# Small work of the attention phase moved from VectorE to GpSimd, and TensorE's unread products taken out

## The chip, the cores and the metric

The kernel runs on one core of one Trainium2 chip. A core has five engines with a queue of instructions each: TensorE (PE, matrix products into PSUM banks), VectorE (DVE), ScalarE (ACT), GpSimd (POOL) and SyncE (SP), which here issues nearly all DMAs. The engines run beside each other and wait for one another through semaphores; each keeps its own order. The metric is the time of one launch on the device, in microseconds (us), as the median of several runs.

## The reference

The kernel computes an attention block with normalised queries and keys, then a feed-forward block with a squared relu, all in float32:

```python
# q, k, v: (8, 12, 448, 64); g_q, g_k: (64,); w_in: (768, 2048); w_out: (2048, 768)
def rmsnorm(x, g):
    return x / np.sqrt(np.mean(x * x, axis=-1, keepdims=True) + 1e-06) * g
scores = np.matmul(rmsnorm(q, g_q), rmsnorm(k, g_k).transpose(0, 1, 3, 2)) / np.sqrt(64)
attn = np.exp(scores - np.max(scores, axis=-1, keepdims=True))
attn = attn / (np.sum(attn, axis=-1, keepdims=True) + 1e-09)
x = np.matmul(attn, v).transpose(0, 2, 1, 3).reshape(3584, 768)
h = np.maximum(x @ w_in, 0.0)
out = h * h @ w_out
```

## The kernel before

The kernel takes two heads at a time (a "pair" `i`; 48 pairs, 6 for each batch). The first 12 pairs (two batches, `alone(i)`) go through attention before any feed-forward product can start; this is the first phase. Afterwards four feed-forward units, of two batches each, run with the attention of later pairs set in between their products. The feed-forward products use a form with 7 products in place of 8, so each weight tile and each x tile also needs sums and differences of its quarters ("quarter sums", "first differences"). The weights come in as words that ACT and DVE split and join (`convert`); the first four tiles of them (two of `w_in`, two of `w_out`) are made in the first phase, by `early`.

The start, before the branch on the size of the gains, and after it (cut):

```python
        gains = psum.tile([P, 1], F32, name="gains")
        nothing = psum.tile([P, P], F32, name="nothing")
        for _ in range(10):
            nc.tensor.matmul(nothing, lhsT=ident, rhs=ident, start=True, stop=True)
        ...
        idle(2)          # products of the identity into bank 5, read by nothing
        turn(0, 1)       # transposes of k, on TensorE
        idle(5)
        turn(0, 0)       # of q, after it has been scaled
        idle(5)
        for x in range(2):
            rows.normalize_first(1, x, new_acc()[:, 0 : 4 * P])
```

Normalising is a sum of squares (`square` on ACT or POOL, `add` on DVE), a power of -1/2 on POOL, and for q a scaling on POOL (line 221), which the next `turn` on TensorE waits for.

The denominators of a pair in the first phase: TensorE adds the weights with columns of ones, into two blocks of 32 rows for each head (line 488), so two partial sums have to be added over partitions:

```python
    def take_sums(i):
        inverse[i] = io.tile([P, S], F32, name="inverse", tag="squares", bufs=1)
        nc.vector.transpose(inverse[i], sums_bank(i))                              # 516

    def invert(i):
        columns = inverse[i].rearrange("p (t n) -> p t n", n=SIDE)
        few = columns[:, :, 0:1]
        if alone(i) or shift:
            other, both = new_few(), new_few()
            for n in range(P // SIDE):
                nc.vector.tensor_copy(out=other[ts(n, SIDE)], in_=few[ts(n ^ 1, SIDE)])   # 525
            nc.vector.tensor_tensor(out=both, in0=few, in1=other, op=ALU.add)             # 526
            few = both
        ...
        nc.vector.reciprocal(out=by, in_=few)                                      # 531
        nc.vector.transpose(columns, by.to_broadcast([P, S // SIDE, SIDE]))        # 532
    # finish(i): xT = values' bank * inverse, on DVE (544); then begin_forms(c) for the second batch
```

Two PSUM banks hold values and sums of the pairs by turns. The visit of a pair in the first phase has two halves, `n` = 0 and 1; `begin` makes two quarter sums and, when it is time, converts a piece of weights:

```python
    def make_sum():
        if sums_to_make:
            to, left, right, op = sums_to_make.popleft()
            next(sum_engines).tensor_tensor(out=to, in0=left, in1=right, op=op)    # 904, DVE and POOL by turns
        elif forms_to_store:
            nc.sync.dma_start(*forms_to_store.popleft())

    early = deque(2 + 2.4 * n for n in range(ahead + 1))     # ahead = 16

    def begin(step):
        for _ in range(2):
            make_sum()
        while early and early[0] <= step:
            early.popleft()
            convert()
            end_join()

    def visit_alone(i, n):
        step = i * 2 * VISITS + 2 * n                        # VISITS = 2
        if n == 0:
            load_v(i)
            weigh_slots(i, n)                                # scores, exponentials (401, 409)
            turn(i + 1, 0); turn(i + 1, 1)
            square(i + 2, 0, new_acc()); square(i + 2, 1, new_acc(), nc.gpsimd)
            begin(step)
            normalize(i + 2, 0)
            attend(i - 1, range(NJ))                         # weights times values (475)
        else:
            weigh_slots(i, n)
            normalize(i + 2, 1)
            begin(step)
            ...
            load_qk(i + 4)
            attend(i - 1, (NJ,))
            add_weights(i - 1, range(NJ + 1))                # 488
            take_sums(i - 1)
            invert(i - 1)
            finish(i - 1)
        begin(step + 1)
```

In the later phases POOL has added up the weights of a pair beforehand, and `denominators(i)` multiplies their sum by ones (505) and calls `take_sums`. It is called from the pair's visit, or, in the first feed-forward unit and for every other pair, half a visit ahead of it:

```python
                    if n and first and x > 1 and i % 2 == 0 and not shift:
                        denominators(i - 1)
                run(COST * x / unit)                         # feed-forward products up to here
                ...
                    visit_among(i, n)                        # denominators(i - 1) here, if not yet made
```

Of the kernel before, what the change touches and what calls it, by code (L numbers as in the profile page):

```python
# [13 lines left out]
F32 = mybir.dt.float32  # L14
# [3 lines left out]
ALU = mybir.AluOpType  # L18
# [3 lines left out]
P = 128  # L22
# [4 lines left out]
SIDE = 32  # L27
# [9 lines left out]
@with_exitstack  # L37
def kernel(
    ctx: ExitStack,
    tc: tile.TileContext,  # L40
    q: bass.AP,
    k: bass.AP,
    v: bass.AP,
    g_q: bass.AP,
    g_k: bass.AP,
    moe_w_in: bass.AP,
    moe_w_out: bass.AP,
    out: bass.AP,
):

    nc = tc.nc
    D = q.shape[3]
    const = ctx.enter_context(tc.tile_pool(name="const", bufs=1))
    wide = const.tile([P, P + D], F32, name="wide")
    ident = wide[:, 0:P]  # L60
    ones = const.tile([P, D], F32, name="ones")
    minus_half = const.tile([P, 1], F32, name="minus_half")
    g = const.tile([P, 1], F32, name="g")
    g_most = const.tile([1, 1], F32, name="g_most")
    bounded = const.tile([1, 1], I32, name="bounded")
    rows = Rows(nc, SimpleNamespace(io=const, small=const), q, k, minus_half)
    with (
        tc.tile_pool(name="early", bufs=1) as early,
        tc.tile_pool(name="gains", bufs=1, space=bass.MemoryType.PSUM) as psum,
        tc.manual_schedule(engines=ENGINES),  # L70
    ):
        g_rows = early.tile([1, 2, D], F32, name="g_rows")
        for n, row in enumerate((g_q, g_k)):
            nc.scalar.dma_start(g_rows[:, n], row.rearrange("(one d) -> one d", one=1))
        rows.load_full(0, 0, nc.sync)
        rows.load_rest(0, 0, nc.scalar)
        rows.load_full(0, 1, nc.sync)
        rows.load_rest(0, 1, nc.sync)
        for x in range(2):
            rows.load_full(1, x, nc.sync)  # L80
        nc.vector.memset(ones, 1.0)
        nc.vector.memset(minus_half, -0.5)
        nc.scalar.activation(early.tile([1, 1], F32, name="some"), ones[0:1, 0:1], AF.Exp)
        make_identity(nc, ident)
        nc.gpsimd.tensor_copy(out=wide[:, P : P + D], in_=ident[:, 0:D])
        nc.vector.tensor_tensor(out=g_rows[:, 0], in0=g_rows[:, 0], in1=g_rows[:, 1], op=ALU.mult)
        nc.vector.tensor_reduce(
            out=g_most, in_=g_rows[:, 0], axis=AX.X, op=ALU.max, apply_absolute_value=True
        )
        nc.vector.tensor_scalar(  # L90
            out=bounded, in0=g_most, scalar1=MOST_G, scalar2=None, op0=ALU.is_le
        )
        gains = psum.tile([P, 1], F32, name="gains")

        nothing = psum.tile([P, P], F32, name="nothing")
        for _ in range(10):
            nc.tensor.matmul(nothing, lhsT=ident, rhs=ident, start=True, stop=True)
        for e in range(2):
            nc.tensor.matmul(
                gains[ds(e * D, D), :], lhsT=g_rows[:, 0], rhs=ones[0:1, 0:1], start=True, stop=True  # L100
            )
        for x in range(2):
            rows.normalize_first(0, x, early.tile([P, 2 * P + 2 * P], F32, name=f"squares{x}"))
        nc.scalar.mul(g, gains, D**-0.5)
    flag = nc.values_load(bounded, min_val=0, max_val=1)
    with tc.If(flag > 0) as either:
        program(tc, rows, v, g, wide, ones, moe_w_in, moe_w_out, out, shift=False)
    with either.Else():
        program(tc, rows, v, g, wide, ones, moe_w_in, moe_w_out, out, shift=True)
# [118 lines left out]
def program(ctx, tc, rows, v, g, wide, ones, moe_w_in, moe_w_out, out, shift):  # L228

    nc = tc.nc  # L230
# [18 lines left out]
    psum = ctx.enter_context(tc.tile_pool(name="psum", bufs=1, space=bass.MemoryType.PSUM))  # L249
# [3 lines left out]
    ident = wide[:, 0:P]  # L253
# [260 lines left out]
    def take_sums(i):  # L514
        inverse[i] = io.tile([P, S], F32, name="inverse", tag="squares", bufs=1)
        nc.vector.transpose(inverse[i], sums_bank(i))  # L516
# [4 lines that stand above are left out]
        new_few = lambda: small.tile([P, S // SIDE, 1], F32, name="few", tag="few", bufs=3)  # L521
        if alone(i) or shift:
            other, both = new_few(), new_few()
            for n in range(P // SIDE):
                nc.vector.tensor_copy(out=other[ts(n, SIDE)], in_=few[ts(n ^ 1, SIDE)])
            nc.vector.tensor_tensor(out=both, in0=few, in1=other, op=ALU.add)
            few = both
        if shift:
            nc.vector.tensor_scalar(out=few, in0=few, scalar1=1e-9, scalar2=None, op0=ALU.add)
        by = new_few()  # L530
        nc.vector.reciprocal(out=by, in_=few)
        nc.vector.transpose(columns, by.to_broadcast([P, S // SIDE, SIDE]))
# [34 lines left out]
    def less(engine, dst, left, right):  # L567
        return lambda: engine.tensor_tensor(out=dst, in0=left, in1=right, op=ALU.subtract)
# [12 lines left out]
    def begin_forms(c):  # L581

        if c < NK:
            b11, b12, t1 = xts.pop((0, c)), xts.pop((1, c)), new_x()
            less(nc.vector, t1, b12, b11)()
            forms[0, c] = {"11": b11, "T1": t1, "T3": b12}
            return
        c -= NK
        b21, b22, t2, t4 = xts.pop((0, c + NK)), xts.pop((1, c + NK)), new_x(), new_x()
        some = forms[0, c]  # L590
        less(nc.vector, t2, b22, some["T1"])()
        less(nc.gpsimd, some["T3"], b22, some["T3"])()
        less(nc.gpsimd, t4, t2, b21)()
        some.update({"21": b21, "22": b22, "T2": t2, "T4": t4})
# [303 lines left out]
    sum_engines = cycle((nc.vector, nc.gpsimd))  # L898

    def make_sum():  # L900

        if sums_to_make:
            to, left, right, op = sums_to_make.popleft()
            next(sum_engines).tensor_tensor(out=to, in0=left, in1=right, op=op)
        elif forms_to_store:
            nc.sync.dma_start(*forms_to_store.popleft())

# [66 lines left out]
# [7 lines that stand above are left out]
# [35 lines left out]
    def visit_alone(i, n):  # L1016
        step = i * 2 * VISITS + 2 * n
        if n == 0:
            load_v(i)
            if i and shift:  # L1020
                attend_all(i - 1)
            weigh_slots(i, n)
            turn(i + 1, 0)
            turn(i + 1, 1)
            square(i + 2, 0, new_acc())
            square(i + 2, 1, new_acc(), nc.gpsimd)
            begin(step)
            normalize(i + 2, 0)
            if i and not shift:
                attend(i - 1, range(NJ))  # L1030
# [4 lines that stand above are left out]
            if in_blocks(i + 2):  # L1035
                store_q(i + 2)
                load_blocks(i + 2, 0)
                load_blocks(i + 2, 1)
            load_qk(i + 4)
            if i and not shift:  # L1040
                attend(i - 1, (NJ,))
                add_weights(i - 1, range(NJ + 1))
                forget(i - 1, range(NJ + 1))
                take_sums(i - 1)
                invert(i - 1)
                finish(i - 1)
            if not alone(i) and not shift:
                additions(i)
        begin(step + 1)

    def put_in_order(i):
        for x in range(2):
# [76 lines left out]
    with tc.manual_schedule(engines=ENGINES):  # L1129
        if shift:  # L1130
            rows.scale(0, 1, nc.gpsimd)
        def idle(number):
            for _ in range(number):
                nc.tensor.matmul(banks[5][:, 0:P], lhsT=ident, rhs=ident, start=True, stop=True)

        idle(2)
        turn(0, 1)
        idle(5)
        turn(0, 0)
        idle(5)  # L1140
        for x in range(2):
            rows.normalize_first(1, x, new_acc()[:, 0 : 4 * P])
        if shift:
# [1 line left out]
        for i in range(len(pairs) + 1):  # L1145
            for n in range(1 if whole(i) else VISITS):
# [8 lines left out]
                if i < last:  # L1155
                    for some in (1, 0) if whole(i) else (1 - n,):
                        turn_among(i + 1, some)
                    if n or whole(i):
                        tasks.append(lambda i=i: load_qk(i + 4))
                    if n and first and x > 1 and i % 2 == 0 and not shift:  # L1160
                        denominators(i - 1)
                run(COST * x / unit)
                if x == unit:
# [43 lines left out]
```

## Time and profile before

| What | Value |
|---|---|
| time, median of 3 runs | 1438.16 us (1435.96 to 1438.75) |
| span of the profiled execution | 1436.9 us |
| first phase: from the start to the first feed-forward product (L663) | 136.5 us |
| x W_in products (L663), busy | 514.6 us |
| products with W_out (L744, two groups of left operands) | 266.5 and 203.9 us |
| scores (L401) and values (L475), busy over the whole run | 162.5 and 102.0 us |
| POOL's power (L206), 96 times | 146.6 us |

A row of the profile's groups has line, engine, operation, output and inputs by the program's names, shape and type, count; then busy time and the mean length of one in ns; then the idle time of the engine just before it and what ended it. "L401" is line 401 of the kernel. PEld is the loading of weights into TensorE, beside its products. A product in float32 shows as two records. The chain of waits is followed back from the last instruction: at each step to what released it.

### The profile page before, as it was taken

How to read it: one execution, taken by the hardware profiler on the slowest of the kernel's cores; microseconds unless marked ns; L12 is line 12 of the kernel's file. 1: busy time of each engine (PE TensorE's matmuls, PEld its weight loads, DVE VectorE, ACT ScalarE, POOL GpSimd, SP SyncE). 2: the span in 40 equal slices, each digit the busy share in tenths (PEclk: the TensorE clock that was granted, in tenths of full speed). 3: DMA queues.
4: the chain of work that ended last, by engine and by line, in shares of the span. 5: the costliest groups of instructions: out<-in, count | busy, mean ns of one | idle time of the engine just before them, and what ended most of it. 6: DMA issues, size and time to landing. Idle time of an engine off the chain costs nothing.

```text
span 1436.9 us, 15452 instructions
## 1 busy us (share of the span) xinstructions
PE 1417.4 (99%) x4976; PEld 694.9 (48%) x4976; DVE 671.4 (47%) x1269; ACT 585.2 (41%) x1102; POOL 646.1 (45%) x568
## 2 busy tenths in 40 slices
PE   9999999999999999999999999999999999999997
PEld 5333444444444445445454544545454455555554
DVE  5997366877868523334242532334243341132313
ACT  6774566557554343432424334341432303212130
POOL 5667654746647654354535644453451502011110
PEclk9999999999999999999999999999999999999999
DMA  5765346666567654534425464344422232313122
GB/s 146 188 192 155 66 119 174 184 181 173 178 193 230 195 135 96 174 88 127 127 52 176 113 209 112 86 141 93 153 70 88 94 153 78 117 48 126 39 88 80
DMA packets 309280, 188.12 MB, mean 131 GB/s; under 512 B 265796, under 2 KB 293316, under 8 KB 300996
## 3 DMA queue, kind: packets, MB, share of 16 engines
q1 hardware_dynamic: 308896, 186.97, 44.5%
q8 instruction: 41, 0.67, 0.2%
q14 instruction: 51, 0.42, 0.1%
q10 hardware_dynamic: 292, 0.07, 0.0%
HBM read 144.57 MB, written 42.40 MB: 130 GB/s over the span
## 4 chain that ended last, share of the span: by engine, by line
PE 93%; DVE 2%; SPq 1%; DMA 1%; ACT 1%; issue 1%; POOL 1%; DVEq 0%; POOLq 0%
PE bank L663 36%; PE bank L744 29%; PE bank L475 10%; PE bank L401 9%; PE bank L715 5%; PE bank L505 2%; PE bank L488 1%; SPq L161 1%; PE bank L366 1%; DVE acc L785 0%; DMA words<-in_moe_w_out_dram 0%; DVE in_sb L882 0%; DVE in_sb L858 0%; DMA qk<-in_k_dram 0%; DVE in_sb L878 0%
## 5 line engine op out<-in xcount | busy, mean ns | idle before, releaser
L663 PE MATMUL bank<-xT,in_sb 128*128 128x448 f32 x1344 | 514.6, 542 | 0.0
L663 PEld LDWEIGHTS bank<-xT,in_sb 128*128 128x128 f32 x1344 | 253.2, 190 | 258.8 <-issue 248.3
L785 DVE TENSOR_TENSOR acc<-acc,bank 128x384 f32<-128x384 f32 x324 | 174.1, 550 | 216.7 <-PE bank L744 173.7
L744 PE MATMUL bank<-out_sb,hid 128*128 128x384 f32 x768 | 266.5, 487 | 0.0
L683 DVE TENSOR_TENSOR hid<-bank,part 128x448 f32<-128x448 f32 x128 | 76.9, 622 | 313.0 <-PE bank L663 310.2
L409 ACT ACTIVATE wT<-bank,rr 128x448 f32<-128x448 f32 x288 | 160.8, 631 | 127.2 <-PE bank L401 80.9
L744 PE MATMUL bank<-out_sb,sums 128*128 128x384 f32 x576 | 203.9, 490 | 3.0 <-DVE acc L785 2.9
L206 POOL TENSOR_TENSOR rr<-ms,minus_half 128x8 f32<-128x8 f32 (+1 forms) x96 | 146.6, 1527 | 112.5 <-DVE ms L199 105.4
L744 PEld LDWEIGHTS bank<-out_sb,hid 128*128 128x128 f32 x768 | 145.7, 190 | 103.3 <-issue 1.4
L428 POOL TENSOR_TENSOR sum<-wT 128x448 f32<-128x448 f32 x72 | 83.8, 1183 | 213.3 <-PE bank L505 213.3
L699 POOL TENSOR_TENSOR sums<-hid 128x384 f32<-128x384 f32 x32 | 32.1, 1002 | 310.4 <-ACT hid L685 310.4
L428 POOL TENSOR_TENSOR sum<-sum,wT 128x448 f32<-128x448 f32 (+1 forms) x144 | 163.7, 1161 | 10.8 <-ACT wT L409 8.1
L401 PE MATMUL bank<-qT,kT 64*128 64x448 f32 (+1 forms) x768 | 162.5, 569 | 0.6 <-ACT wT L409 0.3
L684 ACT ACTIVATE hid<-hid 128x448 f32<-128x448 f32 x128 | 73.3, 573 | 189.7 <-DVE hid L683 189.7
L744 PEld LDWEIGHTS bank<-out_sb,sums 128*128 128x128 f32 x576 | 108.0, 190 | 86.7 <-DVE acc L785 7.5
L670 ACT COPY part<-bank 128x448 f32<-128x448 f32 x128 | 67.6, 528 | 177.4 <-PE bank L663 177.4
L401 PEld LDWEIGHTS bank<-qT,kT 64*128 64x128 f32 (+1 forms) x768 | 54.4, 172 | 102.2 <-issue 66.4
L475 PE MATMUL bank<-wT,vt 128*64 128x448 f32 x480 | 102.0, 546 | 0.0
L516 DVE STREAM_TRANSPOSE inverse<-bank 128x448 f32<-128x448 f32 x48 | 30.9, 643 | 119.4 <-PE bank L505 111.8
L715 PE MATMUL bank<-out_sb,hid 128*128 128x384 f32 x256 | 85.6, 488 | 0.0
L339 ACT ACTIVATE qT<-qT,g 128x448 f32<-128x448 f32 x34 | 22.6, 665 | 143.0 <-DVE qT L337 143.0
L685 ACT ACTIVATE hid<-hid 128x448 f32<-128x448 f32 x128 | 73.8, 577 | 4.1
(87 smaller groups left out, 1189.5 us busy)
## 6 DMA issues: line engine op xcount, KB each, us to landing
out_sb<-out_forms SPq DMA_DIRECT2D x24, 1536.0 KB, 9.5
in_sb<-in_forms SPq DMA_DIRECT2D x24, 1344.0 KB, 6.1
words<-in_moe_w_in_dram SPq DMA_DIRECT2D x32, 384.0 KB, 3.8
words<-in_moe_w_out_dram SPq DMA_DIRECT2D x32, 384.0 KB, 3.8
out_forms<-out_sb SPq DMA_DIRECT2D x8, 1536.0 KB, 6.8
in_forms<-in_sb SPq DMA_DIRECT2D x8, 1344.0 KB, 6.0
qk<-in_q_dram SPq DMA_DIRECT2D x96, 96.0 KB, 3.0
qk<-in_k_dram SPq DMA_DIRECT2D x96, 96.0 KB, 2.7
```

The lines of the kernel that those rows point to most:

```text
L206: self.nc.gpsimd.tensor_tensor(out=self.rr[i][:, x, 0 : self.count(i)], in0=ms, in1=self.minus_half.to_broadcast(list(ms.shape)), op=ALU.pow,)
L401: nc.tensor.matmul(sc[some], lhsT=turned[p, 1][r, keys], rhs=turned[p, 0][r, :], start=True, stop=True,)
L409: nc.scalar.activation(new_weights((i, m), e), sc, AF.Exp, scale=rows.rr[i][:, 1, 2 * m + e : 2 * m + e + 1],)
L428: nc.gpsimd.tensor_tensor(out=sums[i, e][some], in0=left[some], in1=weights[key_of(i, m), e][some], op=ALU.add)
L475: nc.tensor.matmul(values_bank(i)[ds(e * D, D), :], lhsT=lasts[i % 2][mine, e, :] if m == NJ else values[i][:, m, e, :], rhs=weights[key_o ...
L663: nc.tensor.matmul(ps, lhsT=w_sb[:, IN.index(left), c, :], rhs=forms[u, c][right], start=first and c == 0, stop=c == NK - 1, skip_group_ch ...
L683: nc.vector.tensor_tensor(out=dst, in0=left, in1=right, op=op)
L684: nc.scalar.activation(dst, dst, AF.Relu)
L685: nc.scalar.activation(dst, dst, AF.Square)
L715: nc.tensor.matmul(ps, lhsT=flat[a][:, t, ds(NT * P, P)], rhs=w_sb[t][:, 2 * a + half, :], start=(a, t) == parts[0], stop=(a, t) == parts[-1],
L744: nc.tensor.matmul(ps, lhsT=lefts[left][:, t, ts(tt, P)], rhs=w_sb[t][:, OUT.index(right), :], start=first and t == 0, stop=t == 1, skip_g ...
L785: nc.vector.tensor_tensor(out=acc, in0=acc, in1=ps, op=ALU.add)
```

## The change

It takes out the products of the identity that nothing reads, at the start. In the first phase, it gives POOL the exchange of the partial sums over partitions and their addition (in `invert`), the quarter sums of the weights while `early` still has entries, and the first differences of the x tiles of the first two batches (`begin_forms`, three times); all of these were VectorE's, or by turns VectorE's and POOL's. So that VectorE has something to do while POOL exchanges, the second `begin` of a visit's second half now stands between `take_sums` and `invert`. In the first feed-forward unit the denominators are made half a visit ahead for every pair, not for every other.

```diff
-        nothing = psum.tile([P, P], F32, name="nothing")
-        for _ in range(10):
-            nc.tensor.matmul(nothing, lhsT=ident, rhs=ident, start=True, stop=True)
...
             for n in range(P // SIDE):
-                nc.vector.tensor_copy(out=other[ts(n, SIDE)], in_=few[ts(n ^ 1, SIDE)])
-            nc.vector.tensor_tensor(out=both, in0=few, in1=other, op=ALU.add)
+                nc.gpsimd.tensor_copy(out=other[ts(n, SIDE)], in_=few[ts(n ^ 1, SIDE)])
+            nc.gpsimd.tensor_tensor(out=both, in0=few, in1=other, op=ALU.add)
...
             b11, b12, t1 = xts.pop((0, c)), xts.pop((1, c)), new_x()
-            less(nc.vector, t1, b12, b11)()
+            less(nc.gpsimd, t1, b12, b11)()
...
-            next(sum_engines).tensor_tensor(out=to, in0=left, in1=right, op=op)
+            engine = nc.gpsimd if early else next(sum_engines)
+            engine.tensor_tensor(out=to, in0=left, in1=right, op=op)
...
                 take_sums(i - 1)
+            begin(step + 1)
+            if i and not shift:
                 invert(i - 1)
                 finish(i - 1)
             if not alone(i) and not shift:
                 additions(i)
-        begin(step + 1)
+        if n == 0:
+            begin(step + 1)
...
-        def idle(number):
-            for _ in range(number):
-                nc.tensor.matmul(banks[5][:, 0:P], lhsT=ident, rhs=ident, start=True, stop=True)
-
-        idle(2)
         turn(0, 1)
-        idle(5)
         turn(0, 0)
-        idle(5)
...
-                    if n and first and x > 1 and i % 2 == 0 and not shift:
+                    if n and first and x > 1 and not shift:
                         denominators(i - 1)
```

## The prediction

> **What bounds the kernel now.** I read the page's busy shares first:
>
> ```profile
> PE 1417.4 (99%) x4976; PEld 694.9 (48%) x4976; DVE 671.4 (47%) x1269; ACT 585.2 (41%) x1102; POOL 646.1 (45%) x568
> ```
>
> TensorE (PE) is busy in 1417.4 of 1436.9 us. All its idle time is 19.5 us, so nothing that merely shortens a wait can bring more than 1.4%. The change takes no product of the reference's arithmetic away and adds none, so I look for what part of those 19.5 us it can reach. The next view is the busy time by stretch; after the bounds and the length its columns are PE, weight loads, DVE, ACT, POOL, granted clock, DMA share, GB/s:
>
> ```profile
> 20.00:40.00 20.00, 19.36 (x121) 7.54 (x120) 14.18 (x36) 16.20 (x32) 13.07 (x11) 1.00 0.63 155
> 40.00:60.00 20.00, 19.67 (x118) 7.14 (x118) 18.83 (x41) 16.32 (x33) 12.40 (x11) 1.00 0.74 207
> 60.00:80.00 20.00, 18.66 (x118) 6.88 (x116) 18.81 (x43) 15.14 (x30) 12.22 (x10) 1.00 0.63 182
> 80.00:100.00 20.00, 20.00 (x122) 7.22 (x118) 18.02 (x41) 15.05 (x30) 12.35 (x11) 1.00 0.58 159
> ```
>
> The reader should see two things. VectorE (DVE) is at 94% from 40 to 80 us, so moving work from it to POOL, at 62%, is sensible. But PE is also at 93 to 100%, so the gain is bounded by what PE loses here. That loss is in the list of waits, where the columns are total us, times and longest (lines from several stretches):
>
> ```profile
> PE bank L366 <- POOL qk L221: 1.3, 1, 1.3
> ...
> PE bank L475 <- DMA lasts<-in_v_dram: 2.9, 1, 2.9
> ...
> PE bank L744 <- DVE acc L785: 1.3, 1, 1.3
> ...
> PE bank L744 <- DVE acc L785: 1.7, 2, 1.1
> ```
>
> The two L744 lines are from 260 to 330 and 330 to 400 us, in the first feed-forward unit. In the first phase I also measure PE's steps in the chain of waits: undisturbed pairs run 8.63 us and 9.54 us, by turns. The starts of the turns in it (20.86, 29.56, 39.10, 47.73, 58.56, 67.19, 78.07, 86.77, 97.07, 106.07, 119.89, 128.66) exceed this by about 1.3 (at 52 us, waiting on ACT), 1.3 (at 78, the L221 wait), 0.7 (at 97), 0.4 (at 106) and 4.3 us (at 107 to 114). That is 8 us in all. The feed-forward unit adds 3.0.
>
> **What the skill says.** The Trainium skill, TensorE: Matmul & The Clock Gate, Part 1, says that the array runs at half rate until about 3.4 us of sustained activity and falls back after such a time idle. The trace agrees in kind:
>
> ```profile
> 1.35 4.64 PE L97 MATMUL nothing<-wide 128*128 128x128 f32 x20 [1.35 <-POOL wide masks.py:199]
> ...
> 7.92 0.85 PE L366 MATMUL bank<-wide,qk 128*128 128x128 f32 x3
> ...
> 10.66 0.49 PE L366 MATMUL bank<-wide,qk 128*128 128x128 f32 x3
> 11.10 1.28 PE L1134 MATMUL bank<-wide 128*128 128x128 f32 x10
> ```
>
> The first 20 records take 4.64/20 = 232 ns each, those at 11.10 take 128 ns: the products of the identity warm the array, by about 10 us. And after the 2.9 us wait at 107 the stretch 110 to 113 us shows a granted clock of 0.54. The Trainium skill, GPSIMD Engine Reference, Engine selection, says that a two-input elementwise operation is about twice as long there as on VectorE; L904, which both run, gives 1062 against 552 ns, 1.9 times. The same page, Instruction dispatch, warns that consecutive Pool instructions do not order the cores, so the exchange between partitions needs waits of its own; no POOL instruction of this trace does it, so that cost is not shown. The Trainium skill, Advanced Engine Details and Errata, DVE Details, says that one of VectorE's ports is shared with POOL; L525 between 161 and 1001 ns for one shape agrees.
>
> **The change part by part.**
>
> ```profile
> L525 DVE COPY few<-inverse 32x14 f32<-32x14 f32 x40 | 8.6, 216 | 1.0
> L526 DVE TENSOR_TENSOR few<-inverse,few 128x14 f32<-128x14 f32 x10 | 2.6, 256 | 0.3
> L904 POOL TENSOR_TENSOR in_sb<-in_sb 128x384 f32<-128x384 f32 x4 | 4.4, 1108 | 2.5 <-DMA qk<-in_q_dram 2.5
> L904 DVE TENSOR_TENSOR in_sb<-in_sb 128x384 f32<-128x384 f32 x4 | 2.6, 660 | 0.0
> ```
>
> 1. Exchange and addition (`invert`, 12 pairs of heads): DVE loses 4 x 216 + 256 = 1.12 us a pair, 13.4 us in all. On POOL I estimate each small one at 0.2 us (its 128x64 copy L85 took 0.24 us; L185 takes 824 ns for 384 elements a partition and 1092 for 512, about 2.1 ns an element, which leaves little but a fixed cost at 14). So POOL gains 5 x 0.2 + 0.1 of waits = 1.1 us a pair, and the chain from sums to xT gets two handovers and POOL's queue in it. In the chain of waits the handovers themselves cost 0.04 us each; being behind a 1.6 us power (L206) or a sum (1.1 us) in POOL's queue is the real cost.
>
> 2. Quarter sums: `early` has 17 entries, of which the last is taken at step 41, and the fourth tile's sums are made after that. So three tiles of the four, 12 sums, are all POOL's in place of 6. DVE loses 6 x 0.66 = 4 us, POOL gains 6 x 1.1 = 6.6 us.
>
> 3. First differences: 3 times 0.63 us (L568 on DVE) become some 1.3 us on POOL.
>
> 4. The second `begin(step + 1)` before the inversion: DVE joins weights (0.35 + 0.56 + 0.56 = 1.5 us) while POOL exchanges. Without it DVE would stand for 1.1 us.
>
> DVE thus gives up 13.4 + 4 + 1.9 = 19 us of the first 130, POOL takes 13 + 6.6 + 3.9 = 24. DVE's 94% falls to some 80, POOL's 62% rises to about 80. PE's products are untouched. What PE wins is part of its waits: of the 1.3 + 1.3 + 0.7 + 0.4 us which hang on ACT, DVE and POOL I give it half, 1.9 us, and take back 0.4 us for the steps in which POOL has four sums to make (near 46 to 50 and 69 to 72 us), where the scaling L221 comes no earlier than now: at 76.55 it now follows a 1.0 us and a 1.1 us sum in POOL's queue (at 69.45 and 71.74), and after the change four. The 4.3 us at 107 I leave as they are: SyncE issued the value load behind the store of out_forms at 97.84, while the DMA engines were 0.98 busy (104 to 107 us), and three of the four sums before that store still take POOL's time. So the first phase: -1.5 us, with a wide margin.
>
> 5. Denominators in the first unit for every pair: `denominators` of five even pairs moves half a visit, about 5 us, ahead. Its transpose (L516, 0.64 us) at 271.12 lies within the jam 270 to 282 us where PE waits 1.3 us for DVE; it goes to an emptier stretch. The one at 396 likewise. The jam at 366 to 374 belongs to a pair already early. Gain 0.6 to 1.2; I take -0.8 us.
>
> 6. No idle products: The 22 products are 44 records; the 20 before 6 us stand in nobody's way, the 24 of L1134 lie between 6.94 and 12.38 us. The turn of q at 10.66 waited for nothing but them (its scaling on DVE ended at 8.86), so it comes 1.7 us earlier. But POOL's chain, power L206 at 9.74 and six memsets to 12.22, lets the next power start at 12.3 in place of 12.89: only 0.6 us is passed on to 20.86 us. Against it stands a cold array: 8 score records take 3.5 in place of 1.77 us, and the turns at 14.86 about 0.5 us more. I put the sum at -0.5, between -1.2 and +1.0.
>
> Sum: -1.5 - 0.8 - 0.5 = -2.8 us; 1438.2 - 2.8 = 1435.4 us.
>
> **The rivals.** First, POOL becomes the bound of the phase: its in-order queue now has the exchange between `take_sums` and the reciprocal, so `finish` gets later, the query's turned copy (L374, behind it on DVE) too, and the next power and L221 with it. For it: POOL is released by DVE in 32.5 us of idle time before L206, so each round trip counts. Against it: that idle time, 3 to 5 us in most steps, is more than the 1.1 us put in. If it holds, PE waits 0.5 to 1 us in each of ten steps: 1438 to 1444 us. Second, DVE's saturation was what made every wait here, also the late store and through it the late value load; then all 8 us and the cold array after them go: 1428 to 1431. Against it: PE steps of 8.63 and 9.54 already recur while DVE is at 94%. Third, the cold start is worse than I think, with the array at half rate until after 20 us; then +1.5 us, 1437 or so.
>
> **Range and chances.** The parts' margins (3, 0.8 and 1.1 us) and the spread of the times before (1435.96 to 1438.75) give 1430.5 to 1439.5 for 8 in 10. Two per cent is 28.8 us, more than PE's whole idle time, so faster by that is nearly impossible, and slower by it would need 2 us more in each of the twelve steps: chances 0.01, 0.98, 0.01.
>
> **What would show it.** In the changed profile, DVE below 17 of 20 us from 40 to 80, POOL at 15 to 17; PE's turns 8.63 and 9.54 us apart with fewer exceptions; the wait for L221 at 78 us still there and the one for the value load near 107 too; the L366 records at half rate at the start, and scores also, yet the turn now at 20.86 no later than 21; the wait L744 near 282 shorter. I am wrong if POOL, not DVE, precedes PE's waits in most steps, if the value load's wait is gone, or if turns before 20 us come over 1 us later.

## The result: 0.9% slower

The changed kernel takes 1451.06 us (1450.59 to 1451.66), the kernel before 1438.45 us in the same comparison: a ratio of 1.0092, with a 95% interval of 1.0074 to 1.0109. The profiled spans are 1449.5 and 1436.9 us.

The busy shares of the page after:

```profile
PE 1416.1 (98%) x4932; PEld 687.4 (47%) x4932; DVE 650.2 (45%) x1200; ACT 586.2 (40%) x1102; POOL 665.6 (46%) x637
```

The span is 12.6 us longer. PE is busy 1.3 us less, although the idle products alone took 4.6 + 4.5 us before: what is left takes some 8 us longer, and the rest of the loss is waiting. The array at half rate is a part of these 8 us (1.6 us in the first scores, and a granted clock of 0.52 from 56 to 59 us and 0.51 from 138 to 141 us); the other part is not accounted for. DVE gave up 21.2 us and POOL took 19.5, where 19 and 24 were planned. The stretches, in the same columns as before the change:

```profile
20.00:40.00 20.00, 19.35 (x122) 7.54 (x121) 11.81 (x26) 16.21 (x32) 15.02 (x21) 1.00 0.64 162
40.00:60.00 20.00, 17.38 (x93) 5.54 (x96) 12.44 (x25) 13.93 (x28) 13.77 (x17) 0.91 0.63 180
60.00:80.00 20.00, 20.00 (x124) 7.39 (x118) 14.19 (x29) 14.36 (x27) 13.97 (x21) 1.00 0.53 118
80.00:100.00 20.00, 18.91 (x116) 7.06 (x114) 15.10 (x29) 14.51 (x27) 15.27 (x22) 1.00 0.71 214
```

DVE falls from 18.8 to 12.4 us of 20 between 40 and 60 us, more than POOL's share of the work explains, and neither engine is full. Nobody is the bound by its sum of work; they wait for each other. The list of waits of the changed kernel from 20 to 136 us, by what waited for what, total, times, longest:

```profile
DVE few L527 <- POOL few L522: 28.0, 10, 6.4
...
PE bank L362 <- POOL qk L217: 6.0, 4, 2.8
PE bank L397 <- DVE qT L370: 2.6, 1, 2.6
PE bank L484 <- DVE xT L540: 2.0, 2, 1.2
```

(Lines have moved by 4: the reciprocal is 527, the addition 522, the scaling of q 217, the copy of the turned query 370.) The first line is the result in one: to be rid of 1.1 us of work in each of ten exchanges, DVE stands 2.8 us before each reciprocal. (Two of the twelve exchanges come after 136 us; over all twelve it stands 34.6 us.) How that comes about is seen in the timelines from 46 us. POOL's, with start, length, line:

```profile
46.21 2.39 POOL L901 TENSOR_TENSOR in_sb<-in_sb 128x384 f32<-128x384 f32 x2
48.56 1.33 POOL L202 TENSOR_TENSOR rr<-ms,minus_half 128x6 f32<-128x6 f32 x1
49.86 2.09 POOL L901 TENSOR_TENSOR in_sb<-in_sb 128x384 f32<-128x384 f32 x2
52.01 0.92 POOL L521 COPY few<-inverse 32x14 f32<-32x14 f32 x4
53.01 0.21 POOL L522 TENSOR_TENSOR few<-inverse,few 128x14 f32<-128x14 f32 x1
```

DVE's:

```profile
46.59 0.63 DVE L512 STREAM_TRANSPOSE inverse<-bank 128x448 f32<-128x448 f32 x1
53.26 0.24 DVE L527 RECIPROCAL few<-few 128x14 f32<-128x14 f32 x1 [6.04 <-POOL few L522]
...
54.76 0.67 DVE L370 TENSOR_SCALAR qT<-bank,g 128x448 f32<-128x448 f32 x1
```

PE's:

```profile
51.03 1.92 PE L397 MATMUL bank<-qT,kT 64*128 64x448 f32 x8
55.58 1.25 PE L397 MATMUL bank<-qT,kT 64*64 64x448 f32 x4 [2.62 <-DVE qT L370]
56.75 1.76 PE L471 MATMUL bank<-wT,vt 128*64 128x448 f32 x4
```

The same place in the kernel before, POOL, then DVE, then PE:

```profile
47.36 1.65 POOL L206 TENSOR_TENSOR rr<-ms,minus_half 128x6 f32<-128x6 f32 x1
48.96 1.00 POOL L904 TENSOR_TENSOR in_sb<-in_sb 128x384 f32<-128x384 f32 x1
49.92 1.04 POOL L185 TENSOR_TENSOR acc<-qk 128x512 f32<-128x512 f32 x1
54.08 1.68 POOL L206 TENSOR_TENSOR rr<-ms,minus_half 128x8 f32<-128x8 f32 x1 [3.12 <-DVE ms L199]
```

```profile
48.40 1.59 DVE L525 COPY few<-inverse 32x14 f32<-32x14 f32 x4
...
52.52 0.68 DVE L374 TENSOR_SCALAR qT<-bank,g 128x448 f32<-128x448 f32 x1
```

```profile
53.35 0.97 PE L401 MATMUL bank<-qT,kT 64*64 64x448 f32 x4 [0.33 <-ACT wT L409]
```

In the changed kernel the sums were transposed by 47.22 us. The exchange of 1.2 us began at 52.01, because four quarter sums and a power stood ahead of it in POOL's queue. DVE, in its own order, could not go past the reciprocal to copy the next pair's query, and the last scores of an even pair (the 64*64 records) need that copy. Then the array is cold:

```profile
56.00:59.00 3.00, 3.00 (x12) 0.52 0.60 134
```

Here the columns after the length are PE's busy time, the granted clock, DMA share and GB/s: 0.52 of full speed after the wait; four L471 records take 1.76 us there, 0.92 us elsewhere. This one step of a pair (turn to turn, 47.61 to 62.31) is 14.7 us long; before it was 10.8, and an undisturbed one is 9.54.

The first feed-forward product starts at 146.63 us, 10.1 us later than before. The other 2.5 us are lost after it, nearly all in the first unit.

### The profile page after: what moved, and what is told of

Its sections match the earlier page's. It is cut to its first block, busy times and chain, and to the rows that moved or that the text cites. A ratio compares the mean times of both kernels' runs of the same rounds, so it can differ in the third digit from the quotient of the medians.

```text
span 1449.5 us, 15380 instructions
## 1 busy us (share of the span) xinstructions
PE 1416.1 (98%) x4932; PEld 687.4 (47%) x4932; DVE 650.2 (45%) x1200; ACT 586.2 (40%) x1102; POOL 665.6 (46%) x637
## 4 chain that ended last, share of the span: by engine, by line
PE 88%; POOL 3%; DVE 3%; issue 2%; SPq 2%; DMA 1%; ACT 1%; POOLq 0%; DVEq 0%; ACTq 0%
PE bank L659 34%; PE bank L740 30%; PE bank L471 9%; PE bank L397 8%; PE bank L711 5%; PE bank L501 2%; POOL rr L202 1%; SPq L157 1%; PE bank L484 1%; POOL in_sb L901 1%; POOL qk L217 0%; POOL few L521 0%; DMA q_rows<-qk 0%; POOL out_sb L901 0%; SPq L166 0%
## 5 line engine op out<-in xcount | busy, mean ns | idle before, releaser
L471 PE MATMUL bank<-wT,vt 128*64 128x448 f32 x480 | 103.0, 550 | 0.0
```

The source lines that it names most:

```text
L471: nc.tensor.matmul(values_bank(i)[ds(e * D, D), :], lhsT=lasts[i % 2][mine, e, :] if m == NJ else values[i][:, m, e, :], rhs=weights[key_o ...
```

## The experiments

The theories at the start were Q, that the place of the exchange in POOL's in-order queue is what costs, and its rivals: R, that the round trip by itself does, and L, that POOL is loaded too much. Each time is a median beside the kernel before on the same chip (1438.7 to 1439.0 us); ratios have 95% intervals.

**One part undone (u_sum).**

```diff
-            engine = nc.gpsimd if early else next(sum_engines)
-            engine.tensor_tensor(out=to, in0=left, in1=right, op=op)
+            next(sum_engines).tensor_tensor(out=to, in0=left, in1=right, op=op)
```

> The changed kernel with the quarter sums back on VectorE and POOL by turns (6 of 12 off POOL). Theory Q (the exchange stands behind quarter sums in POOL's in-order queue, VectorE stands before the reciprocal, and the query's copy behind it comes late): of the 10 us that the first phase lost, 5 to 7 come back, 1444 to 1446 us, and VectorE's 6.0 us wait at 47 us falls under 3. Theory R (the round trip to POOL itself, behind the power alone, costs about 1 us in each step): 1 to 3 us come back, 1448 to 1450.

Measured: 1446.58 us, 1.0055 (1.0038 to 1.0072). The first feed-forward product starts at 140.9 us, 5.8 us sooner than in the changed kernel. DVE's wait at 47 us is 2.93 us. Both are as Q expected, the more so as only six sums of 1.1 us went from POOL; the time itself is 0.6 us above Q's range. But DVE's waits for the exchange still sum to 26.5 us up to 136 us, so the total of that line is not by itself the loss: which step it falls in matters.

**The exchange back on VectorE (u_ex).**

```diff
-                nc.gpsimd.tensor_copy(out=other[ts(n, SIDE)], in_=few[ts(n ^ 1, SIDE)])
-            nc.gpsimd.tensor_tensor(out=both, in0=few, in1=other, op=ALU.add)
+                nc.vector.tensor_copy(out=other[ts(n, SIDE)], in_=few[ts(n ^ 1, SIDE)])
+            nc.vector.tensor_tensor(out=both, in0=few, in1=other, op=ALU.add)
```

> The changed kernel with the exchange and addition back on VectorE, all quarter sums still on POOL, the second begin still ahead of the inversion. Theories Q and R alike: VectorE no longer waits for POOL, 8 to 10 us come back, 1441 to 1443. Theory L (POOL is simply loaded too much by the sums and differences, and its scaling of q comes late whoever exchanges): only 3 to 5 us, 1446 to 1448, and PE still waits over 4 us in all for the scaling between 60 and 140 us.

Measured: 1441.8 us, 1.0021 (1.0014 to 1.0028); first feed-forward product at 137.7 us. All quarter sums are still POOL's here, and PE waits 2.1 us for the scaling from 60 to 140 us, where L asked for over 4. So L has little left: the sums harm when the exchange is behind them.

**The exchange alone (only_ex), on the kernel before, with the second `begin` ahead of it.**

```diff
-                nc.vector.tensor_copy(out=other[ts(n, SIDE)], in_=few[ts(n ^ 1, SIDE)])
-            nc.vector.tensor_tensor(out=both, in0=few, in1=other, op=ALU.add)
+                nc.gpsimd.tensor_copy(out=other[ts(n, SIDE)], in_=few[ts(n ^ 1, SIDE)])
+            nc.gpsimd.tensor_tensor(out=both, in0=few, in1=other, op=ALU.add)
...
+            begin(step + 1)      # between take_sums and invert, and no longer behind them
```

> The kernel before with two parts of the change alone: exchange and addition on POOL, and the second begin ahead of the inversion. Theory Q: VectorE still waits for POOL over 20 us in all, since a power and up to two quarter sums stand ahead of the exchange; 4 to 7 us slower than before, 1443 to 1446. If the exchange harms only together with POOL's extra sums: within 2 us of before.

Measured: 1443.13 us, 1.0032 (1.0021 to 1.0044), with 24.9 us of waits for the exchange up to 136 us. At the lower edge of what Q expected. The order of `begin` is in this run too, so the 4.2 us are not shown to be the exchange's alone.

**Both undone (u_sumex): the two diffs of u_sum and u_ex.**

> The changed kernel with both the quarter sums and the exchange as before; left of the change are the differences on POOL, the order of begin, the denominators and no idle products. Theory Q: only the denominators cost anything, 1 to 2.5 us over before, 1440 to 1441. If the order of begin harms by itself (VectorE's joins ahead of the inversion): 3 us or more over before.

Measured: 1442.06 us, 1.0022 (1.0013 to 1.003). This is what u_ex measured, so without the exchange the quarter sums on POOL cost nothing that can be seen. It is 3.1 us over before: some 1 us more than Q expected, and just at the 3 us that the other answer asked for. The denominators alone cost 1.6 us (below); whether the order of `begin` or the differences on POOL add the other 1.5 us is left open, as the intervals overlap.

**The same work in another order (q_first).** Nothing changes engines against the changed kernel.

```diff
-            begin(step)                    # second half of a visit
+            begin(step, 0 if i else 2)     # no quarter sums
...
-            begin(step + 1)
+            begin(step + 1, 0 if i else 2)
             if i and not shift:
                 invert(i - 1)
+                for _ in range(4):
+                    make_sum()
                 finish(i - 1)
```

> The changed kernel with the same operations on the same engines; only, in a visit's second half, the quarter sums are given to POOL behind the exchange in place of ahead of it. Theory Q (place in POOL's queue): VectorE's 6.0 us wait at 47 us falls to 3 or less, the first phase gets 4 to 6 us shorter, 1445 to 1447 us. Theory L (POOL's sum of work): POOL does just as much, so within 1.5 us of 1451.

Measured: 1443.76 us, 1.0037 (1.0024 to 1.005), 7.3 us less than the changed kernel with the same operations on the same engines; the first feed-forward product starts 6.6 us sooner, at 139.99 us. This is the run that decides between Q and L. One sign of Q failed: DVE's wait at 47 us fell to 3.99 us, not to 3. The waits for the exchange up to 136 us, in the columns used above (over all twelve exchanges they are 26.8 us):

```profile
DVE few L527 <- POOL few L522: 23.2, 11, 4.0
```

Not all of the 7.3 us is due to the order. In the profiles of this run and of the next two, the span ends 6.2 us after the last product; in all the other profiles, before and after among them, it ends 7.9 to 8.1 us after it. What makes these 1.7 to 1.9 us is not shown; they lie behind all of TensorE's work, and the three edits share the new order of the sums. Up to the last product the profile is 5.7 us shorter than that of the changed kernel (1435.7 for 1441.4), still far more than the 1.5 that L allowed.

**The exchange ahead of the power too (x_first), without the denominators' part.**

```diff
-            normalize(i + 2, 1)            # add, then power on POOL
+            rows.add(i + 2, 1)             # the power comes below
...
                 invert(i - 1)
+                rescale(i + 2, 1)          # power for k
+                for _ in range(4):
+                    make_sum()
                 finish(i - 1)
```

(Cut: the two changed `begin` calls of q_first, which are in this run too, and the denominators' line; pairs whose loads wait for that power keep their order.)

> The changed kernel without the denominators' part, and in a visit's second half POOL gets the exchange ahead of both the power for k and the quarter sums; all the moved work stays on POOL. Theory Q in its strongest form (only what stands ahead in POOL's queue harms): VectorE's waits for POOL fall under 15 us, and the time is that of before or less, 1435 to 1440. If the handover itself costs: 1441 to 1444.

Measured: 1437.94 us, 0.9997 (0.9989 to 1.0006): no loss any more that can be measured, with all of the moved work still on POOL; without the 1.7 us won at the end, I estimate it at 0.7 us over before. So R, the round trip by itself, can hold little of the loss. DVE's waits for the exchange fell to 14.5 us up to 136 us, but over all twelve exchanges they are 18.0, more than the 15 of Q's strongest form.

**The same with the quarter sums by turns (x_first_alt): x_first and the diff of u_sum.**

> As x_first, but the quarter sums on VectorE and POOL by turns as in the kernel before. Theory Q: within 1.5 us of x_first. If POOL's sum of work is what is left (its scaling late): 1 to 3 us faster than x_first.

Measured: 1434.8 us, 0.9971 (0.9962 to 0.998): faster than both kernels, by 4.2 us against the kernel before, of which some 1.7 are those at the end. POOL's, DVE's and PE's lines at the same place as above:

```profile
46.48 1.31 POOL L900 TENSOR_TENSOR in_sb<-in_sb 128x384 f32<-128x384 f32 x1
47.85 0.90 POOL L521 COPY few<-inverse 32x14 f32<-32x14 f32 x4
48.83 0.22 POOL L522 TENSOR_TENSOR few<-inverse,few 128x14 f32<-128x14 f32 x1
49.01 1.32 POOL L202 TENSOR_TENSOR rr<-ms,minus_half 128x6 f32<-128x6 f32 x1
```

```profile
49.09 0.24 DVE L527 RECIPROCAL few<-few 128x14 f32<-128x14 f32 x1 [1.60 <-POOL few L522]
...
50.90 0.67 DVE L370 TENSOR_SCALAR qT<-bank,g 128x448 f32<-128x448 f32 x1
```

```profile
50.85 1.94 PE L397 MATMUL bank<-qT,kT 64*128 64x448 f32 x12
```

The query is copied at 50.90 in place of 54.76 us, in time for its scores, and even sooner than in the kernel before, where it was copied at 52.52. The twelve score records, in two groups of eight and four before, now run without a break, and the step from turn to turn is 9.54 us long (47.42 to 56.96). Of POOL's sum of work, the 3 us between x_first and this one is what L keeps.

**The query's copy ahead of the inversion (late_pool), denominators as before.**

```diff
             turn(i + 1, 0)
             turn(i + 1, 1)
+            if i > 1 and not shift:
+                invert(i - 2)
+                finish(i - 2)
```

(Cut: the old place of both calls, which these pairs no longer use.)

> The changed kernel, denominators ahead for every other pair again (1450.0 us so), and the inversion and the product of a pair moved behind the turn of the visit after: VectorE copies the turned query before it waits for POOL. Theory Q in full (the harm goes through the query's copy that stands behind the reciprocal in VectorE's queue): the wait of the scores for the query's copy is gone and the first phase is 7 to 10 us shorter, 1440 to 1443. If the harm goes through the late x tile (its PSUM bank is wanted by the next sums) or POOL's late scaling: under 4 us, over 1446.

Measured: 1447.39 us, 1.0059 (1.0043 to 1.0076), not 1440 to 1443. A miss for Q in full, and what the other answer expected: 2.6 us are won, under 4. The wait of the scores for the copy is gone, and most of its time is lost elsewhere (waits of PE, 60 to 145 us):

```profile
PE bank L362 <- POOL qk L217: 8.3, 4, 2.8
PE bank L484 <- DVE xT L540: 2.6, 2, 1.4
```

So the query's copy is one door of several. While DVE stands, all that is behind it comes late: sums of squares, through them POOL's powers and scalings, and through these the next turns. In these runs it helped more to let the exchange start sooner, or to take it back.

**The same move on the kernel before (late_dve).**

> The kernel before with the same move of the inversion behind the next turn, exchange and sums as they were. If the 1.3 us wait at 52 us of the kernel before is the query's copy too: it goes, 1 to 3 us faster than before, 1436 to 1438. If VectorE's sum of work is what counts there: within 0.7 us of before.

Measured: 1442.76 us, 1.003 (1.0017 to 1.0042): slower, a miss for both answers. PE's waits for the scaling grew from 2.3 to 5.2 us, and at 109 us, where the kernel before waits 2.9 us for the value load, it waits 3.7 us. The wait at 52 us did go (the twelve score records run without a break from 51.73 us), so it was the query's copy; but what was won there was lost elsewhere, 1.2 us of it at 48 us, where PE waits for DVE. The order before was the better one.

**Denominators: undone (u_den), and alone (only_den).** The edit is the last line of the change, out of the changed kernel or into the kernel before.

> The changed kernel with the denominators ahead for every other pair again. The feed-forward products of the first unit lose 2.2 us from their first to their last against the kernel before. If the denominators ahead cost this: 1448.9 us and no drift in the first unit. If it is the late first phase that shifts loads against products: no change, 1451.

> The kernel before with the denominators half a visit ahead for every pair of the first unit, nothing else. If they cost what the changed kernel loses in that unit: 1 to 2 us slower, 1440 to 1441, with a wait of their products for ScalarE's exponentials of 0.7 to 1 us. If that loss comes from the shifted loads: within 0.5 us of before.

Measured: 1450.01 us, 1.0075 (1.0058 to 1.0092), and 1440.32 us, 1.0012 (1.0006 to 1.0019). They cost 1.6 us alone. Within the change the medians differ by 1.0 us and the intervals overlap: u_den lies between its two answers, and its profile still loses 1.5 us after the first feed-forward product. From that product to the first of the second unit (the 337th of 1344 records) the six kernels that have the denominators ahead take 2.0 to 3.2 us longer than the kernel before, the others from 1.0 us less to 1.3 us more. In every kernel that has them the products of the denominators wait for exponentials, for 0.4 to 1.0 us; no kernel without them shows such a wait. PE, then ACT, of the changed kernel:

```profile
275.12 0.97 PE L501 MATMUL bank<-sum,ones 128*64 128x448 f32 x4 [0.83 <-ACT wT L405]
```

```profile
270.20 0.56 ACT L841 ACTIVATE words<-words 128x384 f32<-128x384 f32 x1 [5.38 <-DMA words<-in_moe_w_out_dram]
...
272.79 2.19 ACT L405 ACTIVATE wT<-bank,rr 128x448 f32<-128x448 f32 x4
```

The sums of a later pair go to bank 3, which is a score bank too. Half a visit ahead, its exponentials may still be in ACT's queue: here they end at 274.98 us, behind a split of words that had waited 5.4 us for its load. That this wait is the whole 1.6 us is not shown; in only_den it is 0.4 us.

**No idle products (only_idle): their lines out of the kernel before.**

> The kernel before with the unread products of the identity taken out and nothing else. If the cold array costs (its scores at 11 us ran at half rate): 0.5 to 1.5 us slower than before, 1439 to 1440. If POOL's chain hides it (the turn at 20.8 us came at the same time in both profiles): within 0.3 us of before, 1438.2 to 1438.7.

Measured: 1438.74 us, 1.0 (0.9991 to 1.0008). Taking them out changed nothing that can be measured, within about 1.3 us. In the changed kernel, PE at the start:

```profile
11.20 3.36 PE L397 MATMUL bank<-qT,kT 64*128 64x448 f32 x8 [1.12 <-DVE qT L370]
20.81 0.55 PE L362 MATMUL bank<-wide,qk 128*128 128x128 f32 x3 [0.65 <-POOL qk L217]
```

The scores ran at half rate, 3.36 for 1.77 us, and the turn after them, which waits for POOL, came at 20.81 for 20.86 us.

A caution on single profiles: in only_den the first phase is that of the kernel before, yet its first feed-forward product came at 134.9 in place of 136.5 us. Starts of that product are used above only where they differ by more.

## Why the prediction was wrong

The prediction was 2.8 us less, and it is 12.6 us more.

- **The sum of the exchange (part 1).** The sizes were right: the small operations take 0.20 us on POOL (197 ns a copy, 216 ns the addition), and the exchange with its waits 1.2 us. The step that failed is the account made of them. I wrote that standing behind a power or a sum "is the real cost", and then put no number on it: I credited half of PE's waits, -1.9 us, and took back 0.4. What the runs show in its place is DVE standing 2.8 us before each reciprocal, up to 6.4, and all of DVE's later work with it. With the order of `begin` the exchange cost 4.2 us (only_ex); with the quarter sums ahead of it the loss is 11.0 (u_den, the change without the denominators).
- **The argument against the first rival.** POOL's 3 to 5 us of idle time in a step was to absorb 1.1 us. It lies at another place in the step: in the kernel before, POOL idles from 50.96 to 54.08 us, waiting for DVE's sums of squares, after the exchange; when the exchange comes up, at 48.40, POOL is in the middle of power and quarter sum. Idle time takes up new work only if it falls when that work is wanted. That rival named the mechanism and was too small, 1438 to 1444 us: it left out the cold array after a wait and the step with four sums.
- **The 1.3 us at 52 us.** I read it as a wait for ACT, as the list of waits has it. The same four records wait for the query's copy in the changed kernel, and before, that copy ended at 53.20 and they began at 53.35 us. Where the copy comes sooner (x_first_alt, late_dve) they follow at once, though ACT's exponentials are not over (in x_first_alt they run from 51.90 to 54.11 us). Had I asked what those 64*64 records read, I would have seen how little time the query's copy has.
- **Quarter sums and differences (parts 2, 3).** Without the exchange behind them, free as far as can be seen. The loss is in what the two parts do to each other and not in the sum of each alone: 4.2 us for one, nothing visible for the other, 11 with both.
- **The order of `begin` (part 4)** was to fill DVE's 1.1 us. It fills 1.5 us where there is a piece to join; the wait was up to 6 us.
- **Denominators (part 5).** -0.8 was +1.6 (only_den). I looked at where DVE's transpose falls and not at whose bank the product writes.
- **Idle products (part 6).** -0.5 was 0.0, within the margin given.
- **The value load at 107 us** was expected to stay. It is gone from the changed kernel's waits: PE came to it at 116.0 us in place of 107.2. As I had written, that was a sign of being wrong.

## What to carry to other kernels

Work that moves from one in-order engine to another, with its consumer still on the first, is not worth its duration but the time from its input to its turn in the other queue, and all that stands behind the consumer pays this. So first move it up in the queue that receives it: the moved work was 0.9% slower with the exchange behind a power and up to four sums, and not measurably slower when the exchange stood ahead of them and the denominators were left alone; with the sums by turns again it was 0.3% faster, 0.2% without what was won at the very end. And parts that are harmless alone are to be looked at together when they share a queue.

## What was not expected of the hardware

Small operations are only some 1.2 times slower on POOL: by medians a 32x14 copy takes 197 ns there and 168 ns on VectorE, the 128x14 addition 216 and 177 ns, where a 128x384 sum takes 1.9 times as long. By means the copy is even: 224 ns on POOL in the changed kernel, 222 on VectorE in the kernel before, where single ones took up to 1001 ns. And the array's fall to half rate is not a matter of the length of the wait alone: in the changed kernel the clock was 0.52 from 56 to 59 us, after a wait of 2.62 us at 53 us, while after one of 2.80 us at 112 us the stretch from 115 to 118 us shows 1.00. Both waits are shorter than the 3.4 us that the prediction quotes.
